# Attention and a gated feed-forward block on one core: the last two steps of a visit interleaved, one copy moved to VectorE, and other columns for the output groups

## The chip, the cores and the metric

The kernel runs on one core of a Trainium2 chip. The metric is the device time of one execution in microseconds. Of the kernel before there are three timed runs, with a median of 448.1 us (446.79 to 451.15), and one profiled execution, which took 449.61 us by its own time; its profile spans 447.8 us.

## The reference

Eight batches of twelve heads attend over 448 positions with 64 elements per head. The result, laid out as 3584 tokens of 768 elements, goes through a feed-forward block with a gate:

```python
scores = q @ k.T / sqrt(64);  attn = exp(scores - max) / sum;  x = attn @ v
g = x @ w_gate                       # 768 -> 1536
h = g * sigmoid(g) * (x @ w_val)
out = h @ w_out                      # 1536 -> 768, float32
```

## The kernel before

**Attention.** Two heads form a pair `pr`; there are 48 pairs, six to a batch. A chunk of a pair is one score tile: two or more matmuls into a PSUM tile of tag `s` (L298, L310, L328) and one exponential on ScalarE (L318, L336) of about 0.92 us. When all chunks of a pair exist, its product with the values is made into PSUM tiles of tag `f` (L354, L389), VectorE divides it (L414, L415), and it is transposed into `X`. Queries, keys and values come in by DMAs issued on GpSimd's queue. From pair 12 on GpSimd copies queries and keys (L207) and DMA transposes issued on SyncE's queue turn them (L209, L213). PSUM has three tiles of tag `s` (two banks each, pool `ps_s`) and two of tag `f` (one bank each, `ps_f`).

**Feed-forward.** A block is half a pair of batches: blocks with an even number have 384 tokens, those with an odd number 512. A block has twelve *steps*, one for each 128 of the 1536 hidden elements. A step is six matmuls for the gate into `gp`, a tanh on ScalarE into `sg` (L531), six matmuls for the value into `vp`, and on VectorE `t = (sg+1)*gp` (L542) and `hts = t*vp` (L545). `ffn1_steps` (L503) is a generator that yields after the gate, in the middle of the value and at the end.

**Output product.** Block 0 is multiplied by `w_out` plainly (`plain_out`, L566, six pieces of 384 columns). The others mostly use a scheme with seven products of blocks in place of eight: `out_group` (L592) handles two token tiles and two sets of 192 columns, 42 matmuls of 192 columns in two stages of 18 and 24. It needs differences of blocks of `w_out` (`out_sums`, L482: 24 operations on VectorE, once, 384 elements each, lines L486 to L489) and of `h` (`h_sums`, L492: four operations of 768 elements for each pair of token tiles, L497 to L500). In stage one ScalarE copies the first product to `p1` (L637), VectorE makes `p15` (L638) and rewrites the second column block of PSUM (L640). Stage two's first product follows that; VectorE takes a result from the same bank (L644) before stage two's last product overwrites it, ScalarE takes the first token tile (L619) and VectorE the last part (L650).

**Order.** All engines run their instructions in the order in which the program issues them. The order is written out by hand. After a start-up, a plan of 53 *visits* runs: a visit issues two or three score chunks, at most two products with values, and then the share of feed-forward work that falls on it (L872 to L951). In blocks 0 and 1 that share is a time budget (`run_budget`, L791); from block 2 on it is a table of (steps, groups, plain pieces) for each of seven visits: `EVEN` and `ODD` (L750, L751). Visits whose table entry has a group run it with one step laid between its stages (`run_group`, L774). A visit with chunks but without a value product is called `bare`; in it the first gate uses a tile of tag `f` and is issued ahead of the group's first stage. Sums wait in a list, `sums`; `run_fv` and `run_group` issue one after a gate, in the middle of a value or at a step's end (L753 to L789). After the last visit the last block's steps run with no attention beside them; then two plain pieces, and then the four groups of the last block, whose eight `h_sums` are issued two at a time between pieces and stages (L964 to L978). The output rows go out on SyncE's queue; those of the last two groups are stored in halves of 192 columns, some on ScalarE's queue (`store`, L550).

Of the kernel before, what the change touches and what calls it, by code (L numbers as in the profile page):

```python
# [39 lines left out]
def kernel(  # L40
# [83 lines left out]
    wo = [consts.tile([128, NFB, OH], FP16, name=f"wo{i}") for i in range(2)]  # L124
# [357 lines left out]
    def out_sums(c):  # L482
        b11, b12, b21, b22 = wo[0][:, c], wo[1][:, c], wo[0][:, NH + c], wo[1][:, NH + c]
        t1, t2, t3, t4 = (t[:, c] for t in Tsum)
        return [
            lambda: nc.vector.tensor_sub(t1, b12, b11),  # L486
            lambda: nc.vector.tensor_sub(t2, b22, t1),
            lambda: nc.vector.tensor_sub(t3, b22, b12),
            lambda: nc.vector.tensor_sub(t4, b21, t2),  # L489
        ]  # L490
# [12 lines left out]
    def ffn1_steps(kk, c0, n, hts, late=None):  # L503
        for fb in range(NFB):

            def group(kind, dst, cbs=range(NCB)):
                for cb in cbs:
                    nc.tensor.matmul(  # L508
                        dst[:, 0:n],
                        lhsT=wslice(kind, fb, cb),  # L510
                        rhs=X[kk][:, cb, ds(c0, n)],
                        start=(cb == 0),
                        stop=(cb == NCB - 1),
                    )

            if gate_small[0]:
                gate_small[0] = False
                gp = ps_f.tile([128, 512], FP32, tag="f", name="gp")
            else:
                gp = ps_s.tile([128, 2, 512], FP32, tag="s", name="gp")[:, 0]  # L520
            split = late and fb == 0
            if split:
                vp = ps_f.tile([128, 512], FP32, tag="f", name="vp")
                group("g", gp, range(NCB - 1))
                late()
                group("v", vp, range(NCB - 1))
                group("g", gp, [NCB - 1])
            else:
                group("g", gp)
            sg = fp.tile([128, 512], FP32, tag="sg", name="sg")  # L530
            nc.scalar.activation(sg[:, 0:n], gp[:, 0:n], AF.Tanh, scale=0.5)  # L531
            yield
            if split:
                yield
                group("v", vp, [NCB - 1])
            else:
                vp = ps_f.tile([128, 512], FP32, tag="f", name="vp")
                group("v", vp, range(NCB // 2))
                yield
                group("v", vp, range(NCB // 2, NCB))  # L540
            t1 = fp.tile([128, 512], FP32, tag="t1", name="t1")
            nc.vector.scalar_tensor_tensor(  # L542
                t1[:, 0:n], sg[:, 0:n], 1.0, gp[:, 0:n], ALU.add, ALU.mult
            )
            nc.vector.scalar_tensor_tensor(  # L545
                hts[:, fb, 0:n], t1[:, 0:n], 0.5 * HS, vp[:, 0:n], ALU.mult, ALU.mult
            )
            yield

    def store(osb, kk, l0, n, m0, w, halves=False, small=None, all_small=False):  # L550
        l = l0
        while l < l0 + n:
            b, j = divmod(l, S)
            turned = D if b + NB * kk < QUAD // NHP else 0
            c, p0 = divmod((j + turned) % S, P)
            m = min(P - p0, l0 + n - l, (MQ if turned and j < MQ else S) - j)
            dst = out[ts(NB * kk + b, S), :].rearrange("(p c) m -> c p m", c=NC)[c, p0 : p0 + m]
            src = osb[l - l0 : l - l0 + m]
            if halves:
                dst, src = (x.rearrange("p (h x) -> p h x", h=2)[:, :, ds(m0, w)] for x in (dst, src))  # L560
            else:
                dst, src = dst[:, ds(m0, w)], src[:, ds(m0, w)]
            (small if small and (all_small or m < 64) else nc.sync).dma_start(dst, src)
            l += m
# [27 lines left out]
    def out_group(kk, c0, hts, t, qw, osb, last=False):  # L592
# [18 lines left out]
        def bb(oh, half):  # L611
            return lambda n: wo[oh][:, half * NH + n, w]
# [4 lines left out]
        def out_part(z, h, n, src):  # L617
            dst = osb[z][:].rearrange("p (h m) -> p h m", h=2)[:, ds(h, n), w]
            return nc.scalar.activation(dst, src.rearrange("p (h m) -> p h m", h=n), AF.Copy, scale=1.0 / HS)  # L619

        def stored(z):
            l0 = c0 + (2 * t + z) * 128
            if last:
                store(osb[z], kk, l0, 128, qw * QW, QW, halves=True, small=nc.scalar if qw else None, all_small=not z)
            elif qw:
                store(osb[z], kk, l0, 128, 0, DM)
# [10 lines left out]
        keep1 = nc.scalar.activation(p1[:], a, AF.Copy, scale=1.0 / HS)  # L637
# [5 lines left out]
        d = osb[1][:, ds(OH + qw * QW, QW)]  # L643
# [3 lines left out]
        row0 = out_part(0, 0, 2, g[:, 0, 0:OH])  # L647
        stored(0)
        apart(product(b, hh(1, y), tt(3)), row0)
        nc.vector.scalar_tensor_tensor(osb[1][:, w], b, 1.0 / HS, p1[:], ALU.mult, ALU.add)  # L650
# [3 lines left out]
    def block(i):  # L654
# [4 lines left out]
        return ffn1_steps(kk, c0, n, hts, late), (kk, c0, hts), n  # L659
# [4 lines left out]
    with tc.manual_schedule():  # L664
# [47 lines left out]
        sums = []  # L712
        steps = []

        def pair_groups(kk, c0, hts, t, last=False):
            osb = []

            def begin(qw):
                if not qw:
                    osb.extend(new_osb() for _ in range(2))  # L720
                return out_group(kk, c0, hts, t, qw, osb, last)

            return [(lambda qw=qw: begin(qw), h_sums(hts, t) if not qw else []) for qw in range(2)]

        def add_block(i, visits):
            f1, own, n = block(i)
            fvq.extend([(f1, NCB * n / 2400.0)] * NFB)
# [4 lines left out]
            if i < 2:  # L732
                if i:
                    ffn2_wait.append(own)
                    sums.extend(f for c in range(NH) for f in out_sums(c))
# [17 lines left out]
        def run_part(last=False):  # L753
            next(fvq[0][0])
            if sums:
                sums.pop(0)()
            if last:
                fvq.pop(0)

        def run_fv():  # L760
            t = fvq[0][1]
            next(fvq[0][0])
            next(fvq[0][0])
            if sums:
                sums.pop(0)()
            run_part(True)
            return 2 * t

        def run_o():
            gen, t = oq.pop(0)  # L770
            next(gen)
            return t

        def run_group(nf, inside=None, gate_first=False):  # L774
            gen = groups.pop(0)[0]()
            for _ in range(nf - 1):
                run_fv()
            if gate_first:
                run_part()
            next(gen)  # L780
            if not gate_first:
                run_part()
# [3 lines left out]
            run_part()  # L786
            run_part(True)
# [3 lines left out]
        def run_budget(budget):  # L791
            while (fvq or oq) and budget > 0:
                budget -= run_fv() if fvq else run_o()
            return budget

        def left():
            return sum(2 * t for _, t in fvq) + sum(t for _, t in oq)
# [66 lines left out]
        def open_products(rests):  # L864
# [3 lines left out]
            return []  # L868

        carry = 0.0  # L870
        after_group = False
        for x, (chunks, todo) in enumerate(plan):  # L872
# [62 lines left out]
            else:  # L935
# [6 lines left out]
                for _ in range(nf):  # L942
                    run_fv()
# [23 lines left out]
        for gen, _ in last_out:  # L967
            for _ in range(2):
                sums.pop(0)()
            next(gen)  # L970
        for pair in final:
            gens = [begin() for begin, _ in pair]
            for stage in range(2):
                for gen in gens:
                    next(gen)
                    for f in sums[:2]:
                        f()
                    sums[:] = sums[2:]  # L978
# [30 lines left out]
```

## Time and profile before

| what | us |
|---|---|
| timed runs, median (lowest to highest) | 448.1 (446.79 to 451.15) |
| profiled execution, its own time | 449.61 |
| its span | 447.8 |
| TensorE matmuls busy | 431.6 (96%), 4456 instructions |
| VectorE, ScalarE, GpSimd busy | 257.5, 224.0, 180.6 |
| TensorE waits on VectorE's `hts` ahead of `acc` | 2.1 in 9 places |
| L542 and L545, each | 0.69 for 512 tokens, 0.55 for 384 |
| L486 to L489 each; L497 to L500 each | 0.35 at the least; 0.55 |

A line of the timeline gives the start in microseconds from the span's start, the duration, the engine, the line of the kernel, the operation, what it writes and reads, and how many like it were merged; a bracket gives the idle time of the engine before it and what ended that. Matmuls overlap at their ends, so the time that a row of them takes is read from its start to the start of the next row: six gate or value matmuls of 512 columns take 1.29 us, of 384 columns 0.97 us, and 0.03 to 0.1 us pass between a VectorE result and the start of the matmul that waited for it.

### The profile page before, as it was taken

What the parts mean: (1) busy time and instruction counts of PE and PEld (TensorE: products, weight loads), DVE (VectorE), ACT (ScalarE), POOL (GpSimd) and SP (SyncE); (2) the same over time, 40 slices, a digit from 0 to 9 for tenths busy, and PEclk for the clock granted to TensorE, in tenths of its full rate; (3) what the DMA queues carried; (4) which work ended last, traced back from release to release, by engine and by line L of the source; (5) the groups of instructions that cost most, each with busy time, mean ns of one, the idle gap of its engine ahead of it and who ended that gap; (6) DMA issues with size and microseconds to landing.
All of it is one profiled execution on the core that took longest, in us unless ns stands there. A gap on an engine that the chain in (4) does not pass through costs nothing.

```text
span 447.8 us, 11019 instructions
## 1 busy us (share of the span) xinstructions
PE 431.6 (96%) x4456; PEld 274.4 (61%) x4456; DVE 257.5 (57%) x608; ACT 224.0 (50%) x335; POOL 180.6 (40%) x299
## 2 busy tenths in 40 slices
PE   7999999799999999999999999999999999999995
PEld 3666565454446676674656676664755778565484
DVE  4665561286878555655457645654457655754552
ACT  7965666356554546454645455545554542222221
POOL 8656724998785536536424463723000000000000
PEclk9999999899999999999999999999999999999998
DMA  9999999999997897974999689944231012202015
GB/s 139 182 199 201 200 180 126 152 190 192 134 140 103 104 138 104 163 94 69 118 119 135 79 116 135 160 95 61 49 98 48 13 47 56 72 1 72 0 37 143
DMA packets 109012, 49.98 MB, mean 112 GB/s; under 512 B 60832, under 2 KB 105632, under 8 KB 108960
## 3 DMA queue, kind: packets, MB, share of 16 engines
q0 software_dynamic: 46832, 24.56, 48.0%
q1 hardware_dynamic: 61792, 24.49, 30.2%
q8 instruction: 35, 0.57, 0.6%
q10 hardware_dynamic: 336, 0.22, 0.2%
q14 instruction: 17, 0.14, 0.1%
HBM read 49.55 MB, written 11.01 MB: 135 GB/s over the span
## 4 chain that ended last, share of the span: by engine, by line
PE 67%; DMA 13%; DVE 8%; ACT 5%; POOL 4%; issue 2%; SPq 0%; DVEq 0%; POOLq 0%
PE gp L508 19%; PE vp L508 17%; PE og L599 15%; PE acc L389 7%; DMA wv<-in_moe_w_val_dram 5%; DMA qkraw<-in_k_dram 5%; PE op L570 4%; PE s L298 3%; ACT E L318 3%; DVE hts L545 2%; DMA wg<-in_moe_w_gate_dram 2%; DVE t L542 2%; POOL qkraw L170 2%; ACT sg L531 1%; DMA qkT<-qk 1%
## 5 line engine op out<-in xcount | busy, mean ns | idle before, releaser
L508 PE MATMUL gp<-X,wg 128*128 128x384 f16 (+1 forms) x576 | 124.9, 353 | 0.0
L508 PE MATMUL vp<-X,wv 128*128 128x384 f16 (+1 forms) x576 | 124.8, 352 | 0.0
L318 ACT ACTIVATE E<-s 128x896 f16<-128x896 f32 x126 | 106.7, 919 | 22.1 <-PE s L298 11.6
L531 ACT ACTIVATE sg<-gp 128x384 f32<-128x384 f32 (+1 forms) x96 | 52.4, 546 | 102.3 <-PE gp L508 97.8
L542 DVE SCALAR_TENSOR_TENSOR t<-sg,gp 128x384 f32<-128x384 f32 (+1 forms) x96 | 59.5, 620 | 66.8 <-ACT sg L531 66.5
L508 PEld LDWEIGHTS <-wv 128*128 128x128 f16 x576 | 56.3, 98 | 52.0
L207 POOL COPY qk<-qkraw 128x512 f16<-128x512 f16 x72 | 43.7, 647 | 94.2 <-DMA qkT<-qk 91.3
L508 PEld LDWEIGHTS <-wg 128*128 128x128 f16 x576 | 53.6, 98 | 45.8 <-issue 2.6
L545 DVE SCALAR_TENSOR_TENSOR hts<-t,vp 128x384 f16<-128x384 f32 (+1 forms) x96 | 59.7, 621 | 10.0
L147 POOL DMA_DIRECT2D vraw<-in_v_dram x72 | 44.2, 642 | 15.4 <-DMA qkraw<-in_k_dram 7.2
L389 PEld LDWEIGHTS <-E 128*128 128x128 f16 (+1 forms) x1152 | 37.4, 96 | 13.7 <-issue 8.3
L389 PE MATMUL acc<-vo,E 128*128 128x65 f16 (+1 forms) x1152 | 43.3, 193 | 2.2 <-DVE hts L545 2.1
L599 PEld LDWEIGHTS <-hts 128*128 128x128 f16 x528 | 44.0, 98 | 2.2 <-issue 1.1
L336 ACT ACTIVATE E<-s 112x896 f16<-112x896 f32 x48 | 40.6, 917 | 7.9 <-PE s L328 7.8
L147 POOL DMA_DIRECT2D qkraw<-in_k_dram x70 | 42.6, 626 | 1.5 <-DMA wv<-in_moe_w_val_dram 0.8
L414 DVE RECIPROCAL R<-acc 128x4 f32<-128x4 f32 x72 | 12.8, 178 | 39.2 <-PE acc L389 39.2
L619 ACT ACTIVATE osb<-og 128x384 f32<-128x384 f32 x22 | 10.8, 490 | 45.6 <-PE og L599 40.8
L298 PE MATMUL s<-qkT 64*128 64x448 f16 x216 | 30.5, 353 | 2.9 <-DMA qkT<-qk 2.1
L415 DVE TENSOR_TENSOR xt<-acc,R 128x256 f16<-128x256 f32 x72 | 30.6, 425 | 2.5
L170 POOL DMA_DIRECT2D qkraw<-in_q_dram x44 | 29.9, 680 | 3.8 <-PE vp L508 1.0
L599 PE MATMUL og<-wo,hts 128*128 128x192 f16 x264 | 29.0, 246 | 0.0
L570 PE MATMUL op<-wo,hts 128*128 128x384 f16 (+1 forms) x192 | 27.4, 297 | 0.4 <-DVE xt L415 0.4
(77 smaller groups left out, 384.8 us busy)
## 6 DMA issues: line engine op xcount, KB each, us to landing
vraw<-in_v_dram POOLq DMA_DIRECT2D x72, 64.0 KB, 4.6
qkraw<-in_q_dram POOLq DMA_DIRECT2D x41, 112.0 KB, 4.1
qkraw<-in_k_dram POOLq DMA_DIRECT2D x68, 64.0 KB, 4.3
wg<-in_moe_w_gate_dram POOLq DMA_DIRECT2D x8, 288.0 KB, 10.0
wv<-in_moe_w_val_dram POOLq DMA_DIRECT2D x8, 288.0 KB, 10.9
wo<-in_moe_w_out_dram POOLq DMA_DIRECT2D x2, 1152.0 KB, 19.8
out_dram<-osb SPq DMA_DIRECT2D x7, 288.0 KB, 5.0
out_dram<-osb SPq DMA_DIRECT2D x6, 336.0 KB, 3.3
```

What stands on the lines that cost most here:

```text
L147: eng.dma_start(dst[ts(s, 64)], rows)
L207: nc.gpsimd.tensor_copy(dst.rearrange("p c h d -> p h c d"), src)
L298: nc.tensor.matmul(s[:, hx, 0:S], lhsT=t[ts(hx, 64), ts(c + low(pr, hx), 128)], rhs=t[ts(hx, 64), ds(NC * 128, S)], start=True, stop=True,)
L318: nc.scalar.activation(e[:, 0 : 2 * S].rearrange("p (h q) -> p h q", h=2), s[:, :, 0:S], AF.Exp, scale=sm_scale)
L336: nc.scalar.activation(e[:, :, 0:S], s[0:P, :, 0:S], AF.Exp, scale=sm_scale)
L389: nc.tensor.matmul(acc[:, ts(j, D + 1)], lhsT=e[rows, ds(hx * S + j * 128, 128)], rhs=Vts[pr % NV][rows, hx, col, 0 : D + 1], start=first, ...
L508: nc.tensor.matmul(dst[:, 0:n], lhsT=wslice(kind, fb, cb), rhs=X[kk][:, cb, ds(c0, n)], start=(cb == 0), stop=(cb == NCB - 1),)
L531: nc.scalar.activation(sg[:, 0:n], gp[:, 0:n], AF.Tanh, scale=0.5)
L542: nc.vector.scalar_tensor_tensor(t1[:, 0:n], sg[:, 0:n], 1.0, gp[:, 0:n], ALU.add, ALU.mult)
L545: nc.vector.scalar_tensor_tensor(hts[:, fb, 0:n], t1[:, 0:n], 0.5 * HS, vp[:, 0:n], ALU.mult, ALU.mult)
L570: nc.tensor.matmul(op[:, 0:w], lhsT=hts[:, fb, ts(ch, 128)], rhs=wo[oh][:, fb, ds(off, w)], start=fb == 0, stop=fb == NFB - 1,)
L599: nc.tensor.matmul(dst, lhsT=lhs(n), rhs=rhs(n), start=first and n == 0, stop=n == NH - 1, skip_group_check=True)
```

## The change

- The steps become objects (`Step`) with methods `gate`, `value(half)`, `gated` (L542) and `finish` (second half of the value, L542 if it isn't made yet, L545).
- `run_pair` issues two steps as gate, gate, value, value: both L542 follow the first half of the first value, the first L545 follows the first value, and the second L545 ends the pair. `run_steps` uses it for the last two steps of a table visit without a group or plain piece, if the next visit isn't bare; `run_budget` uses it when the budget left is between one and two steps, in blocks with 512 tokens.
- A pair issues one sum in a table visit and two in a budget visit; two single steps issued four before. Single steps in a budget visit issue three where they issued two. The first eight operations of `out_sums` are issued at the last two plain pieces of block 0.
- In bare visits VectorE makes `p1` in place of ScalarE.
- A group takes 384 neighbouring columns (one half of `w_out`) in place of 192 of each half. The halves of `w_out` are one tile, the operands of `out_sums` are two rows of 192 elements, and the last stores write 384 neighbouring columns; of the last group, the first token tile goes out on ScalarE's queue and the second on SyncE's.
- The eight `h_sums` of the last block are issued four ahead of each of the last two plain pieces, all ahead of the groups.

```diff
-        b11, b12, b21, b22 = wo[0][:, c], wo[1][:, c], wo[0][:, NH + c], wo[1][:, NH + c]
-        t1, t2, t3, t4 = (t[:, c] for t in Tsum)
+        b11, b12, b21, b22 = (wo_all[:, :, f, ts(i, QW)] for f in (c, NH + c) for i in range(2))
+        t1, t2, t3, t4 = (t[:, c].rearrange("p (h m) -> p h m", h=2) for t in Tsum)
...
         def bb(oh, half):
-            return lambda n: wo[oh][:, half * NH + n, w]
+            return lambda n: wo[qw][:, half * NH + n, ts(oh, QW)]
...
-                store(osb[z], kk, l0, 128, qw * QW, QW, halves=True, small=nc.scalar if qw else None, all_small=not z)
+                store(osb[z], kk, l0, 128, qw * OH, OH, nc.sync if z or not qw else nc.scalar)
...
-        keep1 = nc.scalar.activation(p1[:], a, AF.Copy, scale=1.0 / HS)
+        if own:
+            keep1 = nc.vector.tensor_scalar_mul(p1[:], a, 1.0 / HS)
+        else:
+            keep1 = nc.scalar.activation(p1[:], a, AF.Copy, scale=1.0 / HS)
...
+        def run_fv(quiet=False, more=0):
+            step = fvq.pop(0)
+            step.gate()
+            add_sum(more)
+            step.value(0)
+            if not quiet:
+                add_sum()
+            step.finish()
+            if not quiet:
+                add_sum()
+            return 2 * step.time
+
+        def run_pair(small=0):
+            one, two = fvq.pop(0), fvq.pop(0)
+            one.gate()
+            two.gate()
+            one.value(0)
+            one.gated()
+            two.gated()
+            one.finish()
+            add_sum(small)
+            two.value(0)
+            add_sum()
+            two.finish()
+            return 4 * one.time
+
+        def run_steps(n):
+            for _ in range(n - 2):
+                run_fv()
+            if n > 1:
+                run_pair()
+            elif n:
+                run_fv(True)
...
         def run_o():
             gen, t = oq.pop(0)
             next(gen)
+            if len(oq) < 2 and not groups and wsums:
+                sums.extend(wsums[:4])
+                wsums[:4] = []
+                add_sum(4)
             return t
...
-                budget -= run_fv() if fvq else run_o()
+                if not fvq:
+                    budget -= run_o()
+                elif len(fvq) > 1 and fvq[0].at[1] and 2 * fvq[0].time < budget <= 4 * fvq[0].time:
+                    budget -= run_pair(1)
+                else:
+                    budget -= run_fv(more=1)
...
-                for _ in range(nf):
-                    run_fv()
+                if no or bare_next(x):
+                    for _ in range(nf):
+                        run_fv()
+                else:
+                    run_steps(nf)
...
         for gen, _ in last_out:
-            for _ in range(2):
-                sums.pop(0)()
+            add_sum(4)
             next(gen)
         for pair in final:
             gens = [begin() for begin, _ in pair]
             for stage in range(2):
                 for gen in gens:
                     next(gen)
-                    for f in sums[:2]:
-                        f()
-                    sums[:] = sums[2:]
```

## The prediction

> **What bounds the kernel now.** I read the page first (span, busy shares, chain), then TensorE's waits, then the timeline at each place that the diff touches.
>
> ```profile
> span 447.8 us, 11019 instructions
> PE 431.6 (96%) x4456; PEld 274.4 (61%) x4456; DVE 257.5 (57%) x608; ACT 224.0 (50%) x335; POOL 180.6 (40%) x299
> PE 67%; DMA 13%; DVE 8%; ACT 5%; POOL 4%; issue 2%; SPq 0%; DVEq 0%; POOLq 0%
> ```
>
> TensorE is busy throughout, and the change removes no matmul: only its pauses can be won. The DMA share of the chain lies before 84 us, which the change leaves as it is.
>
> ```profile
> PE acc L389 <- DVE hts L545: 2.1, 9, 0.3
> PE s L298 <- DMA qkT<-qk: 2.1, 1, 2.1
> PE og L599 <- DVE osb L644: 0.9, 1, 0.9
> ```
>
> So the prize is a few microseconds, in pieces under 1.1. Four kinds of place matter.
>
> **Three-step visits of EVEN tables with sums still waiting** (at 134, 237 and 340 us). The end of the first one:
>
> ```profile
> 140.21 0.55 DVE L497 TENSOR_TENSOR qkraw<-hts 128x768 f16<-128x768 f16 x1
> 140.68 0.55 DVE L542 SCALAR_TENSOR_TENSOR t<-sg,gp 128x384 f32<-128x384 f32 x1
> 141.28 0.37 PE L298 MATMUL s<-qkT 64*128 64x448 f16 x2 [0.36 <-DVE t L542]
> 141.33 0.55 DVE L545 SCALAR_TENSOR_TENSOR hts<-t,vp 128x384 f16<-128x384 f32 x1
> 141.93 1.11 PE L389 MATMUL acc<-vo,E 64*128 64x65 f16 x31 [0.28 <-DVE hts L545]
> ```
>
> The reader sees a sum ahead of the last L542; the third score waits for its tile, then `acc` for L545. From the first score (140.36) to the long `acc` row 1.57 us pass, in the two later visits 1.29. As a pair, both L542 end before the last value does; VectorE runs the second step's L545 from about 139.60 (after an L542 that starts at 139.03), one sum, and the last L545 from 140.75 to 141.30. `acc` starts at 141.35: 0.99 after the first score. Gain 0.58 + 0.30 + 0.30 = **1.2 us**.
>
> **But three sums move on.** These visits issued six sums and now issue three. Of the block's eight, the next visit, which has a group, gets three in place of two, and its third falls between the step's L545 and the group's L644:
>
> ```profile
> 146.88 0.56 DVE L545 SCALAR_TENSOR_TENSOR hts<-t,vp 128x384 f16<-128x384 f32 x1
> 147.35 0.35 DVE L644 SCALAR_TENSOR_TENSOR osb<-og,p 128x192 f32<-128x192 f32 x1
> 147.80 0.66 PE L599 MATMUL og<-qkraw,hts 128*128 128x192 f16 x6
> ```
>
> L644 ends at 147.70, and the stage's last product at 147.80 overwrites what it reads. TensorE follows a VectorE result by some 0.05 us, so 0.05 is spare. One sum of 768 elements moves what follows it by 0.59 (L498 to L499 at the end go from 424.90 to 425.50). So 0.54 is lost, three times: **-1.6 us**. The last two sums go into a visit of two steps where VectorE sits idle 0.73 before each L542: nothing.
>
> **The other pairs.** In the three-step visits at 170 and 273 us (no sums left) L545 starts at 175.79, held by L542, while the last value ended at 175.38; with 0.20 from matmul to reader (a tanh starts at 174.61 behind a gate that ends at 174.41) it could start at 175.58. Gain 2 x 0.21 = **0.4**. In block 1 the budget (4.39 us a visit against 2.56 a step) gives five pairs and two single steps. There L545 starts 0.33 behind the value's end (113.59 against 113.26); at 0.20 a pair wins 0.13, 0.65 for five. Against that: a pair issues its L545, two sums and the second L545 inside one value of 1.29 us (0.60 + 0.31 + 0.31 between starts, 0.04 spare). Four of the 24 `out_sums` took 0.72 to 0.80 instead of 0.35, and these four overlap GpSimd's copies (one at 94.02 the copies from 94.43 on). The first pair's two sums would fall at 94.9 and 95.2, beside the same copies: two long ones, at 0.35 each less what is spare: -0.6. The second single step (122 us) issues a third sum ahead of an L542 that VectorE already delays: -0.35. Together **-0.3**, between -3.8 (all ten sums long) and +0.65. That the operands of `out_sums` become two rows of 192 I cost at nothing: a copy of 512 elements into rows of 64 (L188) took 0.28 at best, so rows that short don't slow VectorE.
>
> **P1 in bare visits** (157, 260, 363 us):
>
> ```profile
> 156.88 0.51 ACT L531 ACTIVATE sg<-gp 128x384 f32<-128x384 f32 x1
> 157.25 0.37 ACT L637 ACTIVATE p<-og 128x192 f32<-128x192 f32 x1
> 157.65 0.36 DVE L638 SCALAR_TENSOR_TENSOR p<-og,p 128x192 f32<-128x192 f32 x1 [2.51 <-ACT p L637]
> 158.53 0.67 PE L599 MATMUL og<-E,hsum 128*128 128x192 f16 x6
> ```
>
> ScalarE comes to `p1` behind three exponentials and a tanh; the value row at 157.28 should end at 158.25, and TensorE waits for L640 until 158.53. VectorE is idle from 155.14. No VectorE copy of 192 elements out of PSUM is in the trace; between the reciprocal's 0.18 and L638's 0.36 I take 0.36. It starts when the first product is done (156.29 + 0.20), L638 follows at 157.0, L640 ends by 157.85, and stage two need not wait: 0.28 + 0.28 + 0.25 = **0.8**; below nothing only if VectorE were late, and it has 0.4 spare. The tables of the Trainium skill speak against it: "VectorE: DVE Perf Modes", section "The TRN2 errata", gives ScalarE 172 + N cycles from PSUM at 1.2 GHz and VectorE 120 + N at 0.96, an estimate of 303 and 325 ns for 192 elements, so the move would lose 0.02 each time. The rows agree on the size (L637 0.34, L638 0.36), but it is the queue in front that costs.
>
> **The end.** Now the sums lie between the groups' operations:
>
> ```profile
> 431.36 0.55 DVE L499 TENSOR_TENSOR hsum<-hts 128x768 f16<-128x768 f16 x1
> 431.95 0.56 DVE L500 TENSOR_TENSOR qkraw<-hts,hsum 128x768 f16<-128x768 f16 x1
> 432.42 0.35 DVE L644 SCALAR_TENSOR_TENSOR osb<-og,p 128x192 f32<-128x192 f32 x1
> 432.83 0.66 PE L599 MATMUL og<-qkraw,hts 128*128 128x192 f16 x6 [0.92 <-DVE osb L644]
> ```
>
> L644 is held by two sums, and a product that could start at 431.74 (431.25 + 0.49) starts at 432.83. All eight sums from 424.32, 0.59 apart, end at 429.0; the first L638 was at 428.84 and slips by 0.2, L640 ends at 429.85, stage two starts at 430.25. The cover is 0.4 us; beyond it the groups slip one for one. Gain **1.1**. Of the stores, the last wait for L650 at 442.86; issue to landing took 3.1. With 768-byte rows at 384 neighbouring columns they are 1536-byte rows, half as many. Stores of whole rows (3072 bytes) land in 2.8 to 5.0 by the medians of the DMA view, those of half rows in 1.8 to 3.1, so I take no gain. SyncE issues one more small store behind L650 (0.4), ScalarE one less; **0**, between -0.5 and +0.5.
>
> **Early sums.** Eight sums now run on VectorE between 83.6 and 86.9, where it sat idle for 6.47 us up to 90.03: nothing, as long as their reads and writes are free. They overwrite key buffers that GpSimd last read for pair 15, by 79.3. Without that cover, 2.8 us of sums would stand ahead of the next division, and TensorE behind it.
>
> **Sum:** 1.2 - 1.6 + 0.4 - 0.3 + 0.8 + 1.1 + 0 = 1.6 us won. The profiled execution of 449.6 would take 448.0. It lay 1.5 above the median; the pauses counted are in every execution, so I take them from the median: **446.5 us**.
>
> **Rivals.** (1) *The moved sums are free.* If the third sum has run before L545 needs VectorE, the -1.6 goes, and if no sum in block 1 is long, +0.65 + 0.3 come: 446.5 - 2.5 = 444.0. For it: VectorE is 57% busy. Against: queues are in order. 0.2. (2) *Slower: sums in block 1's pairs run beside GpSimd's copies.* GpSimd is busy 44.2 of the 50 us from 84 on. If all ten are long, the second L545 comes 0.62 late in five visits and the single step loses 0.75: -3.8 in place of -0.3, 450.0. It decides from about six long sums of ten. For it: the four long ones; against: four of 24. 0.12. (3) *Waits follow tiles, not slices.* Then the first plain piece at 66.21 waits for the second half of `w_out`, issued at 49.31 and landing in 23.3, at 72.6. Of the 6.4 lost, later waits for DMAs (0.74 at 74.22, 2.09 at 81.15) swallow 2.8: 3.6 lost, 450.1. Against: loads into one raw tile run beside reads of others. 0.05. (4) *The pauses only move*: a later wait on VectorE takes each one's place, 448.1. 0.08.
>
> The granted clock was 0.94 between 75 and 84 us and 0.98 in the 50 us after, around the 2.09 wait; 24 plain matmuls took 5.7 there and 3.9 at 423 us. A front that waits differently is worth 1.8 either way. The skill's page "TensorE: Matmul & The Clock Gate", section "What's actually happening", says that the rate halves after at least one idle window of some 3.4 us; by it no new pause here is long enough, which leaves the sum as it is. The row shows it behind 2.1 us, still four times my longest new pause.
>
> **Numbers.** Forecast 446.5, chance 0.55; its own terms give 445 to 448. One per cent (4.5 us) is about what a measurement of this kernel tells from no change. Rival 1 reaches 443.6 or less in some of its cases, and with it the front's 1.8: 0.13 faster. Rivals 2 and 3 pass 452.6 only with a slow front: 0.07. Range 443.4 (rival 1 and part of the store's gain) to 449.8 (just short of rivals 2 and 3).
>
> **What would show it.** Right: the third score after the three-step visits waits for nothing, 0.99 to `acc`; a wait of about 0.5 on L644 in the three group visits behind them; stage two straight behind the value in bare visits; the last groups without a gap, ending near 441.3. Wrong: long L486 to L489 between the two L545 of block 1's pairs, a plain piece that starts late at 66 us, or no wait on L644.

## The result, and the profile after

The changed kernel takes 444.77 us (median of nine runs, 442.25 to 447.02); nine runs of the kernel before, beside them, have a median of 448.70 (446.79 to 451.15). The ratio is 0.9917, with an interval of 0.9888 to 0.9946: 3.7 us won, between 2.4 and 5.0. The forecast was 446.5, 1.6 below the median shown then. The sign came out; the gain is more than twice the forecast.

The profiled execution took 446.76 by its own time. The page of the kernel after: its span, the engines' busy times, and the shares of the chain that ended last.

```profile
span 445.0 us, 11025 instructions
PE 430.9 (97%) x4456; PEld 274.9 (62%) x4456; DVE 263.3 (59%) x611; ACT 222.9 (50%) x332; POOL 180.2 (40%) x299
PE 74%; DMA 13%; DVE 4%; POOL 4%; issue 2%; ACT 1%; SPq 0%; DVEq 0%; POOLq 0%
```

TensorE's busy time is what it was (431.6), and VectorE's share of the chain has halved. VectorE itself is busier by 5.8 us, of which three copies for `p1` make 1.1; the groups of its operations show most of the rest: the 24 `out_sums` took 13.2 in place of 10.3, the `h_sums` 0.4 more.

TensorE's waits in the kernel after (what waited, for what, us in total, times, longest):

```profile
PE acc L390 <- DVE hts L561: 3.0, 4, 1.1
PE s L299 <- DMA qkT<-qk: 1.7, 1, 1.7
...
PE og L610 <- DVE osb L657: 0.4, 1, 0.4
```

Of nine short waits of `acc` for `hts`, 2.1 us in all, five are gone; but four remain and sum to 3.0, the longest 1.1. Something got better and something got worse. To see where, I measured the same stretches in both traces, from one landmark (the first score of a visit) to the next. L561 is the L545 of before, L657 the L644, L500 the L499.

| stretch | before | after | difference | forecast |
|---|---|---|---|---|
| start to block 1's first score | 88.53 | 87.37 | -1.16 | 0, or 1.8 either way |
| block 1 | 43.96 | 45.87 | +1.91 | +0.3 |
| three-step EVEN visit, group visit and the visit ahead, three times | 21.52, 20.98, 20.98 | 20.83, 20.92, 20.69 | -1.04 | +0.4 |
| three-step visits at 170 and 273 us | 14.98, 14.98 | 14.78, 14.78 | -0.41 | -0.4 |
| bare visits with a group, three times | 6.61, 6.61, 6.58 | 6.35, 6.35, 6.37 | -0.73 | -0.8 |
| last groups, first product to last matmul | 14.86 | 13.85 | -1.01 | -1.1 |
| last VectorE result to the span's end | 4.99 | 5.04 | +0.05 | 0 |

The rest, 0.5, is two waits of the profile before that fell differently. Now the places.

**The pair in a table visit.** Timeline of the kernel after, TensorE's and VectorE's rows (start, duration, engine, line, operation):

```profile
140.13 0.55 DVE L561 SCALAR_TENSOR_TENSOR hts<-t,vp 128x384 f16<-128x384 f32 x1
140.60 0.55 DVE L500 TENSOR_TENSOR hsum<-hts 128x768 f16<-128x768 f16 x1
140.99 0.74 PE L299 MATMUL s<-qkT 64*128 64x448 f16 x6
141.09 0.56 DVE L561 SCALAR_TENSOR_TENSOR hts<-t,vp 128x384 f16<-128x384 f32 x1
141.56 1.25 PE L390 MATMUL acc<-vo,E 64*128 64x65 f16 x32
```

No bracket stands on the score or on `acc`: neither sits idle for more than the 0.15 below which the timeline shows none. From the first score on it is 0.57 to the end of the scores, and the first matmul of `acc` follows at once. `acc` is two tiles, one for each head; the second matmul of the row, the first into the second tile, starts at 141.70, 0.05 behind the end of the last L561 (141.65). So `acc` still follows that L561, 0.71 behind the first score where the forecast had 0.99, and TensorE sits idle for next to nothing. Watch the starts on VectorE: 0.47 from L561 to the sum, 0.49 from the sum to L561, although each takes 0.55. They do not depend on each other and overlap.

**The sum that moved** into the group visit behind it:

```profile
146.53 0.55 DVE L561 SCALAR_TENSOR_TENSOR hts<-t,vp 128x384 f16<-128x384 f32 x1
147.00 0.55 DVE L499 TENSOR_TENSOR hts<-hts 128x768 f16<-128x768 f16 x1
147.47 0.35 DVE L657 SCALAR_TENSOR_TENSOR osb<-og,p 128x192 f32<-128x192 f32 x1
147.87 0.66 PE L610 MATMUL og<-qkraw,hts 128*128 128x192 f16 x6
```

L657 starts 0.94 behind L561 where it had started 0.47 behind it, and the last product starts 0.30 later than it could (147.08 + 0.49). The forecast wait is there, and smaller than forecast (0.54). At 249 us it is 0.53: there a sum ahead of it, beside a GpSimd copy, took 0.78.

**P1 in a bare visit:**

```profile
157.05 0.36 DVE L648 TENSOR_SCALAR p<-og 128x192 f32<-128x192 f32 x1 [1.80 <-PE og L610]
157.35 1.14 PE L513 MATMUL vp<-X,wv 128*128 128x384 f16 x6
157.93 0.36 DVE L653 SCALAR_TENSOR_TENSOR og<-p,og 128x192 f32<-128x192 f32 x1
158.35 0.66 PE L610 MATMUL og<-E,hsum 128*128 128x192 f16 x6
```

VectorE had been idle for 1.80 us when the first product came; its copy takes 0.36, the value assumed. Stage two starts 1.00 behind the value's first matmul, where it started 1.25 behind it before: nothing is waited for.

**The end:**

```profile
429.17 0.35 DVE L657 SCALAR_TENSOR_TENSOR osb<-og,p 128x192 f32<-128x192 f32 x1
429.36 0.66 PE L610 MATMUL og<-wo,hsum 128*128 128x192 f16 x6
429.85 0.66 PE L610 MATMUL og<-qkraw,hts 128*128 128x192 f16 x6
```

L657 is done at 429.52, 0.33 ahead of the product that overwrites what it reads; the wait of 0.92 of before is gone.

**Block 1**, where the time was lost (timeline of the kernel after; one pair, VectorE, GpSimd and TensorE):

```profile
93.56 1.33 POOL L208 COPY qk<-qkraw 128x512 f16<-128x512 f16 x2
...
93.72 1.39 DVE L487 TENSOR_TENSOR E<-wo 128x384 f16<-128x384 f16 x1
...
95.15 0.36 DVE L488 TENSOR_TENSOR E<-wo,E 128x384 f16<-128x384 f16 x1
...
95.42 0.68 DVE L561 SCALAR_TENSOR_TENSOR hts<-t,vp 128x512 f16<-128x512 f32 x1
...
96.16 1.11 PE L390 MATMUL acc<-vo,E 64*128 64x65 f16 x31 [1.08 <-DVE hts L561]
```

The pair's first sum starts 0.16 behind a pair of GpSimd copies and ends 0.22 behind them: 1.39 us for an operation that takes 0.35 alone. The pair's second L561 stands behind it, and TensorE waits 1.08 for that. The second pair loses 1.12 in the same way (a sum of 1.56 at 101.80), a later one 0.58 to two sums of 0.61 and 0.76 from 113.41 on; with 0.20 elsewhere these are the 3.0 above. This is the second rival's mechanism, in three pairs instead of all five, and a full hit costs about twice what I had for a whole pair's two sums.

### The profile page after: what moved, and what is told of

Same layout as the page of the kernel before. It is cut to its first block, busy times and chain, and to the rows that moved or that the text cites. A ratio compares the mean times of both kernels' runs of the same rounds, so it can differ in the third digit from the quotient of the medians.

```text
span 445.0 us, 11025 instructions
## 1 busy us (share of the span) xinstructions
PE 430.9 (97%) x4456; PEld 274.9 (62%) x4456; DVE 263.3 (59%) x611; ACT 222.9 (50%) x332; POOL 180.2 (40%) x299
## 4 chain that ended last, share of the span: by engine, by line
PE 74%; DMA 13%; DVE 4%; POOL 4%; issue 2%; ACT 1%; SPq 0%; DVEq 0%; POOLq 0%
PE gp L513 21%; PE vp L513 20%; PE og L610 16%; PE acc L390 8%; DMA qkraw<-in_k_dram 5%; PE s L299 5%; DMA wv<-in_moe_w_val_dram 4%; PE op L581 4%; DMA wg<-in_moe_w_gate_dram 2%; POOL qkraw L171 2%; PE s L311 1%; DMA qkT<-qk 1%; ACT E L319 1%; DVE hts L561 1%; POOL vraw L182 1%
## 5 line engine op out<-in xcount | busy, mean ns | idle before, releaser
L513 PE MATMUL gp<-X,wg 128*128 128x384 f16 (+1 forms) x576 | 123.3, 353 | 0.0
L513 PE MATMUL vp<-X,wv 128*128 128x384 f16 (+1 forms) x576 | 123.2, 352 | 0.0
L561 DVE SCALAR_TENSOR_TENSOR hts<-t,vp 128x384 f16<-128x384 f32 (+1 forms) x96 | 59.5, 620 | 8.9 <-PE vp L513 0.8
L610 PEld LDWEIGHTS <-hts 128*128 128x128 f16 x528 | 44.0, 98 | 2.1 <-issue 1.1
L610 PE MATMUL og<-wo,hts 128*128 128x192 f16 x264 | 29.0, 246 | 0.0
L610 PEld LDWEIGHTS <-hsum 128*128 128x128 f16 x300 | 25.7, 98 | 2.3
```

The lines of the kernel that those rows point to most:

```text
L513: nc.tensor.matmul(dst[:, 0:n], lhsT=wslice(kind, self.fb, cb), rhs=X[kk][:, cb, ds(c0, n)], start=(cb == 0), stop=(cb == NCB - 1),)
L561: nc.vector.scalar_tensor_tensor(self.hts[:, self.fb, 0:n], self.t1[:, 0:n], 0.5 * HS, self.vp[:, 0:n], ALU.mult, ALU.mult)
L610: nc.tensor.matmul(dst, lhsT=lhs(n), rhs=rhs(n), start=first and n == 0, stop=n == NH - 1, skip_group_check=True)
```

## Experiments

Two theories for the long sums. *Place*: a sum is long when it meets GpSimd's copies, whatever its operands, and costs something because it stands between the two L561 of a pair. *Form*: the new operands of `out_sums`, two rows of 192 elements in place of 384 in a row, make it long. And for the gain: it is the sum of the edits' own stretches, each to be undone alone. Kernels are named by what is undone or added. Since the front's time changes by chance from run to run, the stretches above decide and the medians stand beside them.

### Budget visits without pairs

All steps of block 1 are single again, each with two sums.

```diff
-                elif len(fvq) > 1 and fvq[0].at[1] and 2 * fvq[0].time < budget <= 4 * fvq[0].time:
-                    budget -= run_pair(1)
                 else:
-                    budget -= run_fv(more=1)
+                    budget -= run_fv()
```

> The changed kernel without pairs in block 1: its twelve steps are issued singly again, two sums a step; everything else as changed. The seven visits of block 1, from the first score of the visit at 88.5 us (before; 87.4 changed) to that at 132.5 (133.2), took 43.96 before and 45.87 changed. Theory 'place': the pairs' two sums stand between the two L561 and wait there for GpSimd's copies, 1.4 to 1.6 us instead of 0.35. Then singles bring the stretch back to 43.8 to 44.2, whatever the form of the operands, and the whole time to about 443.0 (444.8 less 1.8). Theory 'form': operands in two rows of 192 make a sum wait for GpSimd wherever it stands; then the stretch stays over 44.6, since sixteen sums stand ahead of an L553 or L561 here too.

Measured: 444.87 (seven runs; ratio 0.9920, 0.9892 to 0.9948). Block 1 took 44.03 in place of 45.87, as it would if the loss of the profile after is that of the pairs with their sums. But the median did not fall (444.87 against 444.77), where 443.0 was expected. The profiled execution, the slowest of the seven with 447.03, had a late front: block 1 began at 89.27, 1.9 later than in the profile after, with the clock low for longer (see the last section); that says nothing of the median. What does came out in the next runs: with the changed code in block 1 unaltered, other executions lose less there than the profile after, or nothing.

### The old columns

The groups take 192 columns of each half again, the operands of `out_sums` are contiguous, the stores go in two rows of 192.

```diff
-        b11, b12, b21, b22 = (wo_all[:, :, f, ts(i, QW)] for f in (c, NH + c) for i in range(2))
-        t1, t2, t3, t4 = (t[:, c].rearrange("p (h m) -> p h m", h=2) for t in Tsum)
+        b11, b12, b21, b22 = wo[0][:, c], wo[1][:, c], wo[0][:, NH + c], wo[1][:, NH + c]
+        t1, t2, t3, t4 = (t[:, c] for t in Tsum)
...
-            return lambda n: wo[qw][:, half * NH + n, ts(oh, QW)]
+            return lambda n: wo[oh][:, half * NH + n, w]
...
-                store(osb[z], kk, l0, 128, qw * OH, OH, nc.sync if z or not qw else nc.scalar)
+                store(osb[z], kk, l0, 128, qw * QW, QW, nc.sync if z or not qw else nc.scalar, halves=True)
```

> The changed kernel with the old columns: a group takes 192 columns of each half again, the operands of the sums of the output weights are rows of 384 neighbouring elements, the last stores are two pieces of 192 columns per row (on the changed kernel's queues). Pairs, early sums, P1 and end as changed. Theory 'form': sums of the output weights beside GpSimd's copies take 0.8 at most again, and block 1's seven visits (45.87 changed, 43.96 before) take 44.0 to 44.6. Theory 'place': they stay at 45.5 to 46.2, with sums of 1.3 to 1.6. The end of the kernel, from the last VectorE instruction to the end of the span (4.99 before, 5.04 changed), stays at 5.0 to 5.4 by both. Time 443.2 by 'form', 444.8 by 'place'.

Measured: 444.93 (ten runs; 0.9931, 0.9893 to 0.9969); block 1 44.36, with sums up to 1.14 long; from VectorE's last result to the end 5.19. That is inside what *form* expected of block 1, but 1.14 is more than the 0.8 that it allowed a contiguous sum, and TensorE waited 0.85 for the L561 behind that sum (95.34). The time of block 1 by itself decides nothing, because the two runs below have rows of 192 and gave 43.99 and 43.32.

### P1 by ScalarE everywhere

```diff
-            gen = groups.pop(0)[0](gate_first)
+            gen = groups.pop(0)[0]()
```

> The changed kernel with P1 made by ScalarE in bare visits again. The three waits of TensorE between the step's value and stage two of the group (157, 260 and 363 us before) come back: from the start of the value row to that of stage two 1.25, 1.25 and 1.22 instead of 1.00, so 0.7 to 0.8 us more in all than the changed kernel. A rival, that VectorE then has time for other work that was late, gives less than 0.4.

Measured: 444.67 (ten runs; 0.9925, 0.9894 to 0.9956). The three bare visits went back to 6.60, 6.60 and 6.57: 0.70 in all, against 0.73 won by the change. The timeline of this kernel shows the old order, `p1` behind the exponentials and the tanh:

```profile
155.36 0.36 ACT L650 ACTIVATE p<-og 128x192 f32<-128x192 f32 x1
155.39 1.14 PE L513 MATMUL vp<-X,wv 128*128 128x384 f16 x6
...
156.22 0.36 DVE L653 SCALAR_TENSOR_TENSOR og<-p,og 128x192 f32<-128x192 f32 x1
...
156.64 0.59 PE L610 MATMUL og<-E,hsum 128*128 128x192 f16 x5
```

Stage two starts 1.25 behind the value's start again. The time of the whole kernel can't show 0.7 us, and did not. Block 1, whose code is that of the kernel after, took 43.99 here, 1.9 less than there: what a pair loses differs from execution to execution.

### Table visits without pairs

```diff
-            for _ in range(n - 2):
+            for _ in range(n):
                 run_fv()
-            if n > 1:
-                run_pair()
-            elif n:
-                run_fv(True)
```

> The changed kernel without pairs in the three-step visits of the tables: their last two steps are single again, with six sums in the visit. In those visits (134, 237, 340 us) the old waits come back (third score behind L553, acc behind L561): from the first score of the next visit to the first og 2.5, 2.3 and 2.3 as before instead of 1.66, so +2.0; in the group visits behind them the wait on L657 goes (-1.1), and in the two visits without sums +0.42 comes back. Sum +1.3 against the changed kernel. The recorded theory of the prediction, in which the two effects nearly cancel, gives 0 to +0.4.

Measured: 445.27 (ten runs; 0.9957, 0.9926 to 0.9987), half a microsecond above the kernel after. The three long stretches took 22.38, 21.33 and 20.98 in place of 20.83, 20.92 and 20.69, and the visits at 170 and 273 us 14.98 again. The timeline shows the waits that the pair had removed:

```profile
138.10 0.55 DVE L553 SCALAR_TENSOR_TENSOR t<-sg,gp 128x384 f32<-128x384 f32 x1
138.70 0.37 PE L299 MATMUL s<-qkT 64*128 64x448 f16 x2 [1.10 <-DVE t L553]
...
139.36 0.41 PE L390 MATMUL acc<-vo,E 64*128 64x65 f16 x8 [0.28 <-DVE hts L561]
```

The first stretch lost 1.54 instead of 0.4, because one of its sums met two GpSimd copies:

```profile
134.49 1.22 POOL L208 COPY qk<-qkraw 128x512 f16<-128x512 f16 x2
134.51 1.61 DVE L500 TENSOR_TENSOR hsum<-hts 128x768 f16<-128x768 f16 x1
```

This sum has contiguous rows of 768 and took 1.61 in place of 0.55, the first sign against *form*. Block 1, again the changed code, took 43.32.

### A family without transposing DMAs

To try further orders I used a family in which queries, keys and attention outputs are copied as they are where the DMAs turned them (pair 11's are turned by TensorE). It leaves out these transposes, so the products are of other numbers. Apart from pair 11's turn (18 matmuls and one VectorE copy more), the engines' work, the steps and their order are unchanged.

```diff
-        nc.sync.dma_start_transpose(
-            dst[:, 0:MQ].rearrange("p (j q) -> p j q", j=KR),
-            xt[:, 0 : 2 * KR].rearrange("p j d -> p (j d)"),
-        )
+        nc.sync.dma_start(dst[:, 0:MQ], xt[:, 0 : 2 * KR].rearrange("p j d -> p (j d)"))
```

The kernel before in this form:

> A family without the transposing DMAs: from pair 12 on the queries, keys and attention outputs go through plain DMA copies of the same tiles, so they aren't transposed, and pair 11 is turned by TensorE; all else is as in the kernel before. Work of the engines is the same, transfers are other. It is the family's base for what TensorE waits for on VectorE: the three-step visits should show 2.3 to 2.5 us from the first score behind them to the first og, the bare visits 1.25 from value to stage two, the end 14.9 from the last groups' first product to the last matmul.

The kernel after in this form:

> The changed kernel in the family without transposing DMAs (queries, keys and attention outputs from pair 12 on copied, not transposed). If the change acts through VectorE's order alone, the terms are those of the two profiles: three-step visits 1.66 (0.6 to 0.9 less each than the family's base), waits of 0.3 to 0.5 on L657 in the group visits behind them, bare visits 1.00, the end 13.8. In all 2.5 to 3.9 less than the base from the first group to the end of the span and block 1 together. Rival: the gain measured on the real kernels came from the transfers' phases, and here less than 1.5 is left.

Measured: 446.21 (eight runs) and 442.43 (two runs, 442.02 to 442.84), a difference of 3.8, like that of the real pair (3.9). The stretches repeat: three long ones 21.70, 21.00, 21.00 against 20.83, 20.70, 20.70; bare visits 6.60 each against 6.35, 6.35, 6.70; the end 14.86 against 13.78. (In the third bare visit VectorE started L638 0.85 behind L636, 0.49 after its end; what held it the trace does not show.) Block 1 took 44.19 and 43.92, so here the pairs lost nothing. And the form of before, with contiguous operands, has a long sum too; its timeline:

```profile
127.77 1.50 DVE L472 TENSOR_TENSOR E<-wo,E 128x384 f16<-128x384 f16 x1
127.82 1.23 POOL L207 COPY qk<-qkraw 128x512 f16<-128x512 f16 x2
```

384 elements in a row, 1.50 us, beside two copies. *Form* falls as told: the old operands meet the same fate.

### No sum ahead of L642 in a group visit

```diff
             step.finish()
-            add_sum()
             if not inside:
```

> The family's changed kernel (nothing transposed from pair 12 on), but a group's step issues no sum at its end; the remaining sums go to the next visit of two single steps. Theory 'moved sum': the three waits on L657 in the group visits (0.30, 0.53, 0.30 in the changed kernel) go and nothing takes their place: 1.1 us less than the family's changed kernel. Rival: in the next visit three sums delay L553 or L561, 0.3 to 0.6 come back there, 0.5 to 0.8 less in all.

Measured: 440.83 (two runs). The three long stretches became 0.30 shorter each (20.53, 20.40, 20.40); what the sums cost elsewhere was 0.05 in each bare visit. That is 0.75 in all, not the 1.1 of the theory: the middle visit lost 0.30 in this family, not 0.53. The rest of the 1.6 between the medians lies elsewhere, most of it in the front: in the two profiles block 1 began 1.45 apart. The timeline of this kernel (L546, L642 and L595 are the L561, L657 and L610 of the kernel after):

```profile
142.34 0.55 DVE L546 SCALAR_TENSOR_TENSOR hts<-t,vp 128x384 f16<-128x384 f32 x1
...
142.82 0.35 DVE L642 SCALAR_TENSOR_TENSOR osb<-og,p 128x192 f32<-128x192 f32 x1
...
143.39 0.58 PE L595 MATMUL og<-qkraw,hts 128*128 128x192 f16 x5
```

L642 ends at 143.17, and the product starts 0.49 behind the one ahead of it (142.90), with no wait. So in this family the moved sum costs 0.30 a visit, by its removal as by its row.

### The last sums between the groups

```diff
-            add_sum(4)
+            add_sum(2)
             next(gen)
...
                     next(gen)
+                    add_sum(2)
```

> The family's changed kernel (nothing transposed from pair 12 on) with the eight sums of the last block issued two at a time between plain pieces and stages, as before. From the first product of the last groups to the last matmul: 13.8 in the changed kernel, 14.9 before. The theory says that only the two sums ahead of L657 matter: 1.0 to 1.1 us come back. Rival, that the early sums delay the first L651 so that part of the gain is lost again: less than 0.7.

Measured: 442.95 (two runs); the end took 14.93 in place of 13.78, 1.15 more, and TensorE's waits have their old row again:

```profile
PE og L595 <- DVE osb L642: 0.9, 1, 0.9
```

### Pairs with their sums first

The sums of a pair go between its two gates, none between its two values.

```diff
             one.gate()
+            add_sum(1 + small)
             two.gate()
             one.value(0)
             one.gated()
             two.gated()
             one.finish()
-            add_sum(small)
             two.value(0)
-            add_sum()
             two.finish()
```

> The family's changed kernel (nothing transposed from pair 12 on) with a pair's sums issued behind the first gate, ahead of both L553, and none between its two L561. Block 1's seven visits took 43.92, 44.32 and 44.42 us in three profiles of this family with the changed order, 44.19 in the family's base, and 45.87, 43.99 and 43.32 on the kernel with its transposes. Theory 'place': a sum that waits for GpSimd now delays only an L553 that has time; the stretch is 43.2 to 43.6 whatever the phase, 0.3 to 1.2 less. Rival 'length': long sums in the new place push L553 past the first value and the stretch stays over 43.9.

Measured: 440.67 (four runs; ratio 0.9834, 0.9798 to 0.9871, to the kernel before with its transposes, to which the family's own base is 0.9955). Block 1 took 43.32, though two sums met the copies. The timeline:

```profile
94.75 1.34 POOL L208 COPY qk<-qkraw 128x512 f16<-128x512 f16 x2
94.86 0.75 DVE L474 TENSOR_TENSOR E<-wo 128x384 f16<-128x384 f16 x1
...
95.54 0.76 DVE L475 TENSOR_TENSOR qkraw<-wo,E 128x384 f16<-128x384 f16 x1
...
97.70 0.69 DVE L546 SCALAR_TENSOR_TENSOR hts<-t,vp 128x512 f16<-128x512 f32 x1
...
98.99 0.69 DVE L546 SCALAR_TENSOR_TENSOR hts<-t,vp 128x512 f16<-128x512 f32 x1 [0.61 <-PE vp L498]
```

Both sums are long, and the second L546 waits for TensorE (0.61), not TensorE for it. The same slow operations, moved to a place with slack, cost nothing: *place* stands, for sums of twice the length. None of 1.4 fell there in this profile or the next, so its rival, that such a one would still cost something, isn't tested; and the changed order had once reached 43.32 too. In a table visit the sum loses nothing there either (20.83, 20.70, 20.69).

### Both edits

> The family's changed kernel with both last edits: a pair's sums behind the first gate, and no sum at the end of a group's step. If they act apart, block 1's seven visits take 43.2 to 43.6, the three stretches of three visits 20.5, 20.4 and 20.4 as with the quiet group alone, and the time is 1.2 to 1.8 under the family's changed kernel (442.4): 440.6 to 441.2. Rival: one edit takes back what the other won, and the time is 441.5 or more.

Measured: 441.05 (four runs; 0.9835, 0.9802 to 0.9868, again to the kernel before). Block 1 43.32, the long stretches 20.54, 20.40, 20.40: both gains are there. The median is no better than with the pair's edit alone; its profile's front was 1.4 later, which no edit touches. From block 1's first score to the span's end the profiles give 359.2 (before), 354.8 (after), 353.7 (sums first) and 353.1 (both). By these stretches the two edits beat the kernel before and the kernel after within the family, with one profile each; on the kernel with its transposes neither was measured.

## Why the prediction was right, and where its sizes were off

**Faster by under one per cent: right** (0.8), and from the places named. That the time fell inside the range is in part luck: the range reached down to 443.4 for rival 1 and a gain of the stores, and what took the time below the forecast was neither as told. Term by term:

- **Table pairs, forecast 1.2.** From the first score to the first `og` or `acc` behind it, 2.52, 2.24 and 2.24 became 1.66 each: 2.0 won. The step that failed is "VectorE runs the second step's L545 ..., one sum, and the last L545 from 140.75": I let the operations follow each other by 0.57 to 0.59, and 0.59 I had read from two sums where one needs the other's result. Independent ones follow by 0.47 to 0.49, so the last L561 ended 0.66 behind the first score, not 0.94, and `acc` with it.
- **Moved sums, forecast -1.6.** The same 0.59 for a sum that shifts L657 by 0.47, and 0.05 spare where there was 0.17: the sums ahead of L542 there had been two of which one reads the other's result, and now are two that don't need each other. Lost were 0.30, 0.53 and 0.30, 1.13 in all; without the sums the 0.30 comes back each time. The two terms together were -0.4 in the forecast and are +1.04 here, +1.47 in the family: this one spacing is most of what the forecast lacked. But 1.04 is the best of four profiles of the kernel itself with this code: those of the first three experiments gave 0.73, 0.83 and 0.46, because their first stretch took 21.29, 21.24 and 21.62 in place of 20.83, with a sum of 0.90 to 0.96 beside GpSimd's work in the group visit and, in the third, one of 1.87 in the pair ahead of it.
- **Other pairs in tables, 0.4:** 0.41, and 0.41 lost when the pairs were undone.
- **P1, 0.8:** 0.73, and 0.70 when undone. The copy took the 0.36 that I had taken between 0.18 and 0.36.
- **The end, 1.1:** 1.01, and 1.15 when undone.
- **Block 1, -0.3:** in six profiles with this code it took 45.87, 43.99, 43.32, 43.92, 44.32 and 44.42, 44.3 in the mean, against 43.96 and 44.19 before. So a mean loss of about 0.2 is near the term, but its working isn't, apart from the rows of 192, which cost nothing by themselves (0.35 alone, as before): I priced a long sum at 0.35 (0.72 to 0.80 in place of 0.35), where one that meets two copies can take 1.4 to 1.6 and cost 1.1, and I placed two long ones in the first pair always, where the phase between GpSimd and VectorE decides how many there are in an execution. The bound of -3.8 for ten long sums was therefore too mild, though nothing near ten was seen.
- **Stores, 0 +-0.5:** from VectorE's last result to the end 4.70 to 5.04 in four profiles with the new rows, 4.99 and 5.19 in the two with the old ones; in the family 4.02 to 4.12 against 4.72. That is some 0.6 in the family; on the kernel itself the means differ by 0.2, less than the 0.34 by which those with the new rows differ among themselves.
- **Early sums, 0:** they ran from 83.16 to 87.1, one of them 1.58 long, and nothing behind them was late.

With block 1's mean the sum is 1.04 + 0.41 + 0.73 + 1.01 - 0.25 = 2.9; it is 2.4 with the 0.46, and 4.0 with the family's 1.47 and 0.6 for the stores. The measured 2.4 to 5.0 holds that.

**Rivals.** The first (moved sums free) is refuted as told: they cost 1.13; but its time of 444.0 was near, from the other side, since it was the pair that gave more. The second (long sums in block 1) happened in three of five pairs of the profiled execution and cost 1.9 there; its forecast of 450.0 as the usual case is refuted by the other five profiles. So one of the signs named for a wrong forecast, long sums between the two L545 of block 1's pairs, did show, and the other terms outweighed it. The third (waits follow tiles) is refuted: the first plain piece is late by no more than all of the front before it (0.78). The fourth (the pauses only move) is refuted by the stretches, which end where the next visit begins. In the profile after, the one for the moved sum is the only new wait in a table visit.

**The front.** It was 1.16 shorter in the one pair of executions; with the four experiments on the kernel itself, block 1 began between 2.6 us earlier and 0.7 later than in the profile before, and two of these five were beyond my 1.8. There is one profile of the kernel before to compare with. The mean granted clocks of the timed runs, 0.996 after and 0.996 to 0.997 in three sets of the kernel before, show no difference; whether the change has a share in the front, no run separates.

## What to carry to other kernels

Background work for a queue should be issued where the queue's next result has slack, not between two results that the bounding engine waits for: there the same operation at twice its length cost nothing. The spacing of operations on an engine is to be read from neighbours that don't depend on each other, if those to be moved don't either; here 0.47 against 0.59 decided between a loss and a gain. Where a chancy front moves the whole time by more than an edit is worth, compare stretches between landmarks behind it, in more than one profile.

## What the runs showed of the hardware that was not expected

**GpSimd's work and VectorE's 16-bit sums.** A sum of 384 elements takes 0.35 alone. Of the 288 in the twelve profiles, 77 took 0.43 to 1.65, and those of 768 up to 1.87 in place of 0.55. GpSimd's copies hardly suffer: in the kernel after, a pair of 512 elements each took 1.17 to 1.40 with a sum beside it and 1.17 to 1.37 without. The ends show an order. In 51 of the 77, the instruction that GpSimd had ended last was a copy, and all of these sums end 0.20 to 0.23 behind that copy's end, as if held until it let go. The sum of the pair after that took 1.39 ended 0.22 behind the second of two copies; the one that took 0.75 with its sums first ended 0.22 behind the first of two (95.40). What lets a sum through between two copies or not, no run shows. Nor are copies needed: 15 of the 77 met none, only GpSimd's DMA issues (0.43 to 0.78), and a few sums beside a copy took 0.35. What is shared between the engines, no run here shows.

**The clock in the front.** Between 77 and 91 us some executions have a low granted clock and others don't. The windows of three kernels (stretch, length, busy time of TensorE, its weight loads, VectorE, ScalarE and GpSimd with instructions, granted clock, DMA share, GB/s); the kernel after:

```profile
77.00:91.00 14.00, 12.21 (x132) 7.15 (x131) 8.38 (x20) 7.02 (x10) 14.00 (x25) 0.88 1.53 154
```

budget visits without pairs:

```profile
77.00:91.00 14.00, 11.01 (x120) 6.51 (x119) 6.58 (x17) 5.25 (x8) 14.00 (x25) 0.76 1.41 149
```

table visits without pairs:

```profile
77.00:91.00 14.00, 12.89 (x143) 7.54 (x142) 7.92 (x23) 8.32 (x12) 14.00 (x25) 1.00 1.49 154
```

TensorE issued 120, 132 or 143 matmuls in the same 14 us, at 0.76, 0.88 or 1.00. At half rate, 0.88 of 14 us is a stretch of some 3.4 us and 0.76 one twice as long. A DMA wait stands ahead of each; in the second kernel's timeline:

```profile
81.11 0.56 PE L299 MATMUL s<-qkT 64*128 64x448 f16 x2 [2.91 <-DMA qkT<-qk]
...
83.40 5.94 PE L581 MATMUL op<-wo,hts 128*128 128x384 f16 x24
```

and in the third's, where the wait was 0.74, the same 24 matmuls took 4.07:

```profile
80.29 0.37 PE L299 MATMUL s<-qkT 64*128 64x448 f16 x2 [0.74 <-DMA qkT<-qk]
...
81.98 4.07 PE L581 MATMUL op<-wo,hts 128*128 128x384 f16 x24 [0.37 <-DVE xt L416]
```

The Trainium skill ("TensorE: Matmul & The Clock Gate", section "What's actually happening") has the rate halved after an idle window of some 3.4 us; the length of the slow stretch agrees with that figure. The waits seen ahead of it are shorter, 1.7 in the kernel after and 2.9 in the second kernel, and here the measurement decides. In the profile with `p1` by ScalarE a wait of 1.20 left the clock at 1.00, as the 0.74 did; what decides between 1.20 and 1.7, no run shows.

The DMA wait isn't all of the front's chance. In the family no DMA wait over 0.15 stands between 60 and 91 us, and block 1 still began at 84.69 to 86.28: in the first 12 us TensorE issued 104 to 106 matmuls in the three profiles that began it before 85 us, 88 in the one at 85.33, and 76 in the two at 86.20 and 86.28 (the kernel after and both edits).
